# A fused attention and MLP kernel: the first two blocks of v loaded in rows of two tokens and put apart on VectorE, with a new plan of the instruction order

## The chip, the core and the metric

The kernel runs on one core of one Trainium2 chip. The metric is the device time of one execution in microseconds (us). Engines: PE is TensorE, DVE is VectorE, ACT is ScalarE, POOL is GpSimd, SP is SyncE. Loads that change fp32 to fp16 on their way are issued by POOL; SP and ACT issue loads and stores that keep the type.

## The reference, cut to what matters

```
q, k, v: (4 batches, 8 heads, 768 tokens, 64) fp32
scores = q k^T / 8; keep key j for query i if j < 4 (a "sink") or 0 <= i - j < 128
a = softmax over the kept keys;  x = a v, heads side by side: (3072 tokens, 512)
h = x w_in              (512 x 2048)
g = h * sigmoid(1.702 h)
out = g w_out           (2048 x 512), fp32
```

## The kernel before, in words

The 3072 tokens are cut into twelve blocks k of 256 tokens, three to a batch. Of each block the work goes through these stages, four head pairs p at a time where heads matter.

- Loads. q and k of block 0 come by SP and ACT and those of block 1 by SP (`load_cast`, L517), in fp32; copies on DVE, ACT or POOL then cast them to fp16. All later q and k come cast by POOL's loads (`load_rounded`, L434). v is loaded by POOL (L458), the weights w_in and w_out by POOL too (`weights`, L394): w_in in four slices of 512 columns, w_out in four of 512 rows. Slices 0 and 1 of w_in come in two halves of the contracted dimension (`HALVED`).
- `front`: transposes of q and k on PE (L555), a copy of them to `qkT` (DVE or ACT), the few sink rows of k copied into `ks16` (L305 by the helper `copy`), and the scores against the sinks on PE (L585) with their exponentials `ats` on ACT (L593). The sink rows of v go to `vs16`.
- `scores`: products on PE (L695), exponentials `at` on ACT (L724), a mask by DVE (L742, L738), or for four of the first eight pairs a bias added on PE (L678).
- `back`: the products with v, here called av (L770, L775), 1/sum (`rcp`, L790) and scaling (`xn`, L792) on DVE, a transpose (L803) and a copy to `xT`.
- `mm1`: x w_in on PE (L843) into one bank for each slice s of 256 columns of h, tanh on ACT (L857), and on DVE the product `gT` (L859), which frees the bank. At most three such banks are in use. In blocks 0 and 1 and the slices that come in halves, the products with the first half of w_in for both 128 columns come first.
- `mm2`: g w_out, for block 0 plainly (L1021) and from block 1 on by a scheme of seven products (L920), for which `sums` forms sums of w_out on DVE. Results are put together in `osb` (L945, L947) and stored by SP.

The order of the instructions on each engine is not that of the code: `Plan.run` makes it beforehand. Every operation has a duration for each engine that may run it, a due time (`prio`), the operations that it waits for, and sometimes a place in PSUM that it must acquire; the planner then sets one operation after another, on the engine that could end it first. Loads have an order of their own, a list of names:

```python
LOADS = ["a0", "a1", "v0", "b1", "v1", "w0", "w1", "a2", "w2", "w3", "v2", "w4", "w6", "w5", "w7"]
```

Here a and b are q and k (b1 the second half of block 1's), v is v, w0 to w3 w_in and w4 to w7 w_out. Each engine works through its queue in order. A load on POOL also takes one of eight completion counters in turn (`LANES`), so its issue waits until the load eight before it has landed. The second half of block 1's q and k is held back by a small POOL memset (`go`, L495) which stands after v of block 0. Until 12 us PE runs products of zeros where it has nothing else (L1089).

v of a block lies in SBUF as `v16`: 128 partitions, two groups j of 128 tokens, eight heads. Even tokens of a group are in partitions 0 to 63 and odd ones in 64 to 127. Each of the four loads of a block moves one group's even or odd tokens, rows of one token and head: 64 fp32 read, 64 fp16 written.

Of the kernel before, what the change touches and what calls it, by code (L numbers as in the profile page):

```python
# [10 lines left out]
FP16 = mybir.dt.float16  # L11
# [3 lines left out]
P = 128  # L15
D = 64
TB = 256
# [27 lines left out]

BEGIN = 850.0

LATE, LATE_FROM = 500.0, 40000.0
PATIENCE, SLACK = 4000.0, 300.0

SHARED = ("mask", "sum", "wt", "cqk", "ks")
ENGINES = ("PE", "ACT", "DVE", "POOL", "SP")
# [2 lines left out]
class Plan:  # L55
# [4 lines left out]
    def op(self, eng, dur, lat, fn, deps=(), prio=0.0, acq=None, rel=(), kind=""):  # L60
        return self.any({eng: (dur, lat)}, lambda _: fn(), deps, prio, acq, rel, kind)
# [143 lines left out]
def kernel(  # L205
# [11 lines left out]
    nc = tc.nc  # L217
    B, H, S, Dh = q.shape
# [13 lines left out]

    SEVEN_FROM, SEVEN_TO = 1, NK

    EARLY = {1: 4, 2: 5, 3: 0}
    HALVES_FROM, HALVES_X_FROM = 4, 3
    V1_BEHIND = None

    SPLIT_TO = 1

    ROUNDED_FROM = 2, 2
    GO1 = None, 1
    VS_ON, VS_AT = "DVE ACT", 12000.0
    QK_NS, V_NS = 1000, 300
    NH = NF // 2
    HM = d_model // 2

# [3 lines left out]
    def ring(name, n, shape, dt):  # L251
        return [pool.tile(list(shape), dt, name=f"{name}{i}") for i in range(n)]
# [15 lines left out]
    qk32 = ring("qk32", RS, (P, 4 * H * D), FP32)  # L268
    qk16 = ring("qk16", RQ, (P, 4 * H * D), FP16)
    v16 = ring("v16", RV, (P, 2, H, EV), FP16)  # L270
    qkT = ring("qkT", RKT, (P, 2, 2, NP, P), FP16)
    at = ring("at", RA, (P, 2, 512), FP16)
    ats = ring("ats", RA, (P, TB), FP16)
# [4 lines left out]
    gT = ring("gT", RG, (P, NF, TB), FP16)  # L278
    sm = ring("sm", RSM, (P, 4, NH, P), FP16)
    osb = ring("osb", RO, (P, d_model), FP32)  # L280
    bank = [psp.tile([P, 512], FP32, name=f"bank{i}") for i in range(8)]

    plan = Plan(8, {"s": 6, "k": 1, "t": 2, "a": 2, "x": 2, "h": RTH, "o": 3})
    op = plan.op
# [10 lines left out]
    def pick(ns, engs):  # L295
        return {e: ns[e] for e in engs.split()}
# [7 lines left out]
    def copy(e, out, in_):  # L304
        {"POOL": nc.gpsimd.tensor_copy, "DVE": nc.vector.tensor_copy, "ACT": nc.scalar.copy}[e](out=out, in_=in_)  # L305
# [48 lines left out]
    o_ones = op("DVE", 250, 350, ones, prio=NEVER + 1, kind="const")  # L354

    o_ks0, o_vs0 = [], []
    for b in range(B):
# [7 lines left out]
        prio = 24000.0 + 300.0 * b if b else NEVER + 0.5  # L365
# [4 lines left out]

    COPY = ["DVE ACT"] * NK

    KS_ON = "POOL ACT", "POOL"

    ISSUE = 700
    o_win, o_wout, o_w = {}, {}, []

    HALVED = 2
    loads = []

    def weights(j, at):
# [18 lines left out]
            (o_win if j < 4 else o_wout)[2 * (j % 4) + n] = got if j < 4 else o_l  # L400

    L = 16600.0
    LOADS = ["a0", "a1", "v0", "b1", "v1", "w0", "w1", "a2", "w2", "w3", "v2", "w4", "w6", "w5", "w7"]

    SLABS = (0, 1, 4, 5, 2, 3, 6, 7)

    def load_at(x):
        if x in LOADS:
            return NEVER + 10 * LOADS.index(x) + 3
        return 10000.0 + (int(x[1:]) - 3) * L + (0.6 if x[0] == "v" else 0)  # L410

    def nominal(k, slot):
        return 9000.0 + k * L + slot * L / 8

    def attention(k, slot):

        return nominal(k - 1, slot) - EARLY.get(k, 0) * L / 8

    o_cqk, o_cv, o_vs, o_T = {}, {}, {}, {}

    def load_rounded(k, es, war):

# [3 lines left out]
        c16 = qk16[k % RQ].rearrange("p (i e h d) -> p i e h d", i=2, e=2, h=H)  # L426
        n = 2 if k <= SPLIT_TO else 1
        for c in range(n):
# [14 lines left out]
    def load(k):  # L443
        b, r = divmod(k, R)
        t0 = r * TB
        war = reuse("qk16", k % RQ)
        if k < max(ROUNDED_FROM):
            load_cast(k, [e for e in range(2) if k < ROUNDED_FROM[e]], war)
        load_rounded(k, [e for e in range(2) if k >= ROUNDED_FROM[e]], war)
        w16 = v16[k % RV]  # L450

        war = reuse("v16", k % RV) + ([o_ks[0, V1_BEHIND]] if k == 1 and V1_BEHIND is not None else [])

        o_cv[k] = []
        for j in range(2):
            for i in range(2):
                src = v[b, :, t0 + P * j : t0 + P * j + P].rearrange("h (a i) d -> i a h d", i=2)[i]
                o = op("POOL", ISSUE, (430 if k < 2 else V_NS,), lambda i=i, j=j, src=src: nc.gpsimd.dma_start(  # L458
                    w16[64 * i : 64 * i + 64, j, :, 0:D], src), war + [o_ones],
                       prio=load_at(f"v{k}"), kind="load")  # L460
                if not loads:
                    o.behind = o_mask0
                loads.append(o)
                o_cv[k].append(o)
        if r == 0:

            o_vs[b] = []
            for t in range(2):
                for i in range(2):
                    to = vs16[64 * t + 32 * i : 64 * t + 32 * i + 2, b, :, i]  # L470
                    fr = w16[64 * t : 64 * t + 2, 0, i::2, 0:E]
                    deps = [o_cv[k][t], o_vs0[b]]
                    if b:
                        o = op("SP", 450, (20,), lambda to=to, fr=fr: nc.sync.dma_start(to, fr), deps,
                               prio=nominal(k - 1, 0), kind="vs")
                    else:

                        o = plan.any(pick({"POOL": (400, 500), "DVE": (220, 320), "ACT": (420, 540)}, VS_ON),
                                     lambda eng, to=to, fr=fr: copy(eng, to, fr), deps, prio=VS_AT, kind="ks")
                    o_vs[b].append(o)  # L480
                    uses("v16", k % RV, o)

    def load_cast(k, es, war16):
        b, r = divmod(k, R)
        sl = k
        t0 = r * TB
        prio = load_at(f"a{k}")
        war = [], []
        if k:

            for c, g in enumerate(GO1):
                if g is None:
                    continue
                h = c * H // 2 * 2 * D
                go = op("POOL", 80, 180, lambda h=h: nc.gpsimd.memset(qk32[sl][0:1, h : h + 1], 0.0),  # L495
                        prio=load_at("b1" if c else "a1") - 0.2, kind="go")
                go.behind = o_cv[0][g]
                war[c].append(go)
        dst = qk32[sl].rearrange("p (e h i d) -> p e h i d", e=2, h=H, i=2)
        lq = {}  # L500
        if k == 0:
            for p in range(NP):
                for e, (eng, dma, src) in enumerate((("SP", nc.sync, q), ("ACT", nc.scalar, k_ap))):
                    def f(p=p, e=e, dma=dma, src=src):
                        dma.dma_start(  # L505
                            dst[:, e, 2 * p : 2 * p + 2],
                            src[b, 2 * p : 2 * p + 2, t0 : t0 + TB].rearrange("h (p i) d -> p h i d", i=2),
                        )
                    lq[p, e] = op(eng, 500, (560,), f, prio=NEVER + 2.5 + p / 8, kind="load")
        else:  # L510
            n = 2
            for c in range(n):
                hs = slice(c * H // n, (c + 1) * H // n)
                for e in es:
                    src = (q, k_ap)[e]
                    def f(e=e, src=src, hs=hs):
                        nc.sync.dma_start(  # L517
                            dst[:, e, hs], src[b, hs, t0 : t0 + TB].rearrange("h (p i) d -> p h i d", i=2)
                        )
                    o = op("SP", 450, (1800 / n,), f, war[c], prio=load_at("b1" if c else "a1") + 0.1 * e, kind="load")  # L520
                    loads.append(o)
                    for p in range(c * NP // n, (c + 1) * NP // n):
                        lq[p, e] = o
        c16 = qk16[k % RQ].rearrange("p (i e h d) -> p i e h d", i=2, e=2, h=H)
        w = 2 if k == 0 else 4
        for h0 in range(0, H, w):
            for e in es:
                def f(eng, h=slice(h0, h0 + w), e=e):
                    copy(eng, c16[:, :, e, h].rearrange("s i h d -> s h i d"), dst[:, e, h])

                ps = range(h0 // 2, (h0 + w) // 2)
                o = plan.any(cast(P * w, "DVE ACT" if not k else "DVE ACT POOL"), f, [lq[p, e] for p in ps] + war16,
                             prio=nominal(k - 1, -7 + h0) if k else NEVER + h0, kind="cqk")
                for p in ps:
                    o_cqk.setdefault((k, p), []).append(o)
# [214 lines left out]
    def back(k, p):  # L750

        b, r = divmod(k, R)
        u = NP * k + p
        base = attention(k, 2 * p)
        h8 = L / 8
# [22 lines left out]
        dur = 2 * 57 + 8 * 31 if r else 6 * 31  # L778
        deps = [*o_m[k, p], *o_cv[k]] + ([o_se[k, p], *o_cv[k - 1], *o_vs[b]] if r else [])
        rc, X = rcp[u % RR], xn[k % RXN]  # L780
        if p == 0:
            o_xT["war", k] = reuse("xT", k % RX)
            o_xT["warn", k] = reuse("xn", k % RXN)
        o_a = op("PE", dur, dur + 166, av, deps, prio=base - 2 * h8, acq=("a", 1), kind="av")
        uses("at", u % RA, o_a)
        if r:
            uses("ats", u % RA, o_a)
# [12 lines left out]
        def xt():  # L800
            ps = f16(o_x)[:, 0:TB].rearrange("d (j s) -> d j s", j=2)
            for j in range(2):
# [3 lines left out]
                 acq=("x", 1), kind="xt")  # L806
        uses("xn", k % RXN, o_x)

        def cx(e):
            to, fr = xT[k % RX][:, p], f16(o_x)[:, 0:TB]  # L810
            if k == NK - 1:
# [6 lines left out]
                               prio=base - 0.8 * h8, rel=[(o_x, 0)], kind="cx")]  # L818
# [311 lines left out]
```

## Time and profile before

| what | us |
|---|---|
| median of 3 runs | 217.72 (217.53 to 218.18) |
| the profiled execution | 218.23 |
| its span, first to last instruction | 216.2 |
| PE busy in it | 210.8 |
| DVE busy | 185.4 |
| ACT busy | 133.1 |
| POOL busy | 86.0 |

The profile is of one execution. A line of the timeline gives the start, the time until the end, the engine, the source line, the operation, what it writes and reads, and the sizes; in brackets stands how long the engine idled before it and what ended that. A line "xN" merges N instructions. PE's matmuls overlap in their pipelines, so their times add up to more than PE's throughput needs. POOL's time holds its DMA issues (L458, L394, L434), 0.7 to 0.9 us each. In the list of DMA issues the last number is the time from issue to landing.

### The profile page before, as it was taken

How to read it: one execution, taken by the hardware profiler on the slowest of the kernel's cores; microseconds unless marked ns; L12 is line 12 of the kernel's file. 1: busy time of each engine (PE TensorE's matmuls, PEld its weight loads, DVE VectorE, ACT ScalarE, POOL GpSimd, SP SyncE). 2: the span in 40 equal slices, each digit the busy share in tenths (PEclk: the TensorE clock that was granted, in tenths of full speed). 3: DMA queues.
4: the chain of work that ended last, by engine and by line, in shares of the span. 5: the costliest groups of instructions: out<-in, count | busy, mean ns of one | idle time of the engine just before them, and what ended most of it. 6: DMA issues, size and time to landing. Idle time of an engine off the chain costs nothing.

```text
span 216.2 us, 6592 instructions
## 1 busy us (share of the span) xinstructions
PE 210.8 (97%) x2680; PEld 181.0 (84%) x2680; DVE 185.4 (86%) x429; ACT 133.1 (62%) x277; POOL 86.0 (40%) x136
## 2 busy tenths in 40 slices
PE   7899999999999999999999999999999999999994
PEld 7568887678888988988888988888889889888883
DVE  5698899998988988988988979889979879878674
ACT  3867695366686775765675775864675865744330
POOL 7979564499996260699300080540000000000000
PEclk9999999999999999999999999999999999999999
DMA  6999999999999498099970099091040031022042
GB/s 179 215 196 179 200 192 205 168 163 166 108 167 165 30 144 77 5 133 170 89 124 3 0 96 125 5 114 36 3 97 3 0 76 28 0 52 49 2 100 97
DMA packets 79734, 21.41 MB, mean 99 GB/s; under 512 B 68184, under 2 KB 76888, under 8 KB 79704
## 3 DMA queue, kind: packets, MB, share of 16 engines
q0 software_dynamic: 71200, 12.59, 73.2%
q1 hardware_dynamic: 7416, 7.88, 13.5%
q10 hardware_dynamic: 1088, 0.52, 0.8%
q8 instruction: 21, 0.34, 0.7%
q14 instruction: 9, 0.07, 0.1%
HBM read 27.26 MB, written 6.29 MB: 155 GB/s over the span
## 4 chain that ended last, share of the span: by engine, by line
PE 92%; DVE 3%; DMA 2%; ACTq 1%; issue 0%
PE bank L843 39%; PE bank L920 31%; PE bank L695 5%; PE bank L775 5%; PE bank L1021 3%; DMA qk<-in_k_dram 2%; PE bank L618 2%; PE bank L770 2%; PE bank L585 2%; PE bank L555 1%; DVE osb L947 1%; PE bank L642 1%; PE bank L803 1%; ACTq L505 1%; PE bank L678 1%; DVE xn L792 1%
## 5 line engine op out<-in xcount | busy, mean ns | idle before, releaser
L843 PE MATMUL bank<-xT,w_in 128*128 128x256 f16 x768 | 103.7, 273 | 0.0
L857 ACT ACTIVATE th<-bank 128x512 f16<-128x512 f32 x96 | 57.6, 604 | 57.9 <-PE bank L843 51.6
L843 PEld LDWEIGHTS <-w_in 128*128 128x128 f16 x768 | 71.9, 98 | 8.9
L859 DVE SCALAR_TENSOR_TENSOR gT<-th,bank 128x512 f16<-128x512 f16 x96 | 64.9, 678 | 10.1 <-ACT th L857 9.8
L724 ACT ACTIVATE at<-bank 128x512 f16<-128x512 f32 (+1 forms) x96 | 49.1, 584 | 1.5 <-PE bank L695 1.1
L458 POOL DMA_DIRECT2D v<-in_v_dram x48 | 33.2, 719 | 30.4 <-PE bank L775 24.8
L920 PEld LDWEIGHTS <-sm 128*128 128x128 f16 x352 | 33.3, 98 | 4.2 <-issue 0.2
L920 PE MATMUL bank<-wt,sm 128*128 128x256 f16 x264 | 36.1, 273 | 0.0
L947 DVE SCALAR_TENSOR_TENSOR osb<-bank,osb 128x256 f32<-128x256 f32 x58 | 23.9, 417 | 11.8 <-PE bank L920 11.8
L920 PEld LDWEIGHTS <-gT 128*128 128x128 f16 x264 | 25.5, 98 | 3.4
L920 PE MATMUL bank<-w_out,gT 128*128 128x256 f16 x176 | 26.1, 273 | 0.0
L738 DVE TENSOR_TENSOR at<-at,mask 128x1024 f16<-128x1024 f16 x30 | 20.5, 683 | 0.2 <-ACT at L724 0.2
L792 DVE TENSOR_TENSOR xn<-bank,rcp 128x256 f16<-128x256 f32 x48 | 20.0, 417 | 0.6
L775 PE MATMUL bank<-v,at 128*128 128x65 f16 x352 | 20.0, 193 | 0.0
L434 POOL DMA_DIRECT2D qk<-in_q_dram x20 | 18.0, 925 | 0.6 <-DMA qk<-in_q_dram 0.5
L434 POOL DMA_DIRECT2D qk<-in_k_dram x20 | 18.0, 923 | 0.7 <-PE bank L843 0.5
L775 PEld LDWEIGHTS <-at 128*128 128x128 f16 x352 | 17.4, 97 | 0.9
L305 POOL COPY ks<-qkT 64x4 f16<-64x4 f16 x26 | 8.1, 313 | 18.6 <-DVE qkT L305 17.6
L890 DVE TENSOR_TENSOR sm<-gT 128x1024 f16<-128x1024 f16 x22 | 15.0, 680 | 0.1
L593 ACT ACTIVATE ats<-bank 128x256 f16<-128x256 f32 x32 | 13.0, 405 | 1.7 <-PE bank L585 1.6
L945 ACT ACTIVATE osb<-bank 128x256 f32<-128x256 f32 x22 | 8.4, 382 | 9.1 <-PE bank L920 9.1
L695 PE MATMUL bank<-qkT 64*128 64x256 f16 x192 | 13.3, 244 | 0.0
(58 smaller groups left out, 224.0 us busy)
## 6 DMA issues: line engine op xcount, KB each, us to landing
out_dram<-osb SPq DMA_DIRECT2D x48, 128.0 KB
v<-in_v_dram POOLq DMA_DIRECT2D x48, 64.0 KB, 5.1
qk<-in_q_dram POOLq DMA_DIRECT2D x20, 128.0 KB, 5.4
qk<-in_k_dram POOLq DMA_DIRECT2D x20, 128.0 KB, 5.6
w_out<-in_moe_w_out_dram POOLq DMA_DIRECT2D x4, 512.0 KB, 11.3
w_in<-in_moe_w_in_dram POOLq DMA_DIRECT2D x4, 256.0 KB, 6.6
w_in<-in_moe_w_in_dram POOLq DMA_DIRECT2D x2, 512.0 KB, 8.9
qk<-in_k_dram ACTq DMA_DIRECT2D x4, 128.0 KB
```

The costliest lines, as they stand in the source:

```text
L434: nc.gpsimd.dma_start(c16[:, i, e, hs], src[b, hs, t0 : t0 + TB].rearrange("h (p i) d -> i p h d", i=2)[i])
L458: o = op("POOL", ISSUE, (430 if k < 2 else V_NS,), lambda i=i, j=j, src=src: nc.gpsimd.dma_start(w16[64 * i : 64 * i + 64, j, :, 0:D], src ...
L695: nc.tensor.matmul(f32(o_b or o_s, 2 * n + i)[:, c : c + w].rearrange("s (j t) -> s j t", t=P), src[d, j, 1, p], T[d, j0:j1, 0, p], start= ...
L724: nc.scalar.activation(out=A[:, i, 0:W], in_=f32(o_b or o_s, 2 * n + i)[:, 0:W], func=AF.Exp, scale=scale)
L738: nc.vector.tensor_tensor(out=a_, in0=a_, in1=m_[:, 2 * P :].unsqueeze(1).to_broadcast((P, 4, 2 * P)), op=ALU.mult,)
L775: nc.tensor.matmul(avp()[:, j, i], A[:, i, c : c + P], src[:, jj, 2 * p + i, 0:E], start=not r and n == 0, stop=n == len(blocks) - 1, skip ...
L792: o_nn = op("DVE", 333, 425, lambda: nc.vector.tensor_tensor(out=X[:, p].rearrange("s j (h d) -> s j h d", h=2), in0=avp()[:, :, :, 0:D], ...
L843: nc.tensor.matmul(f32(holder[0])[:, bass.ts(e, TB)], w_in16[:, c, bass.ts(Fi, P)], X[:, c], start=(c == 0 and not (halved and e)), stop=( ...
L857: o_t = op("ACT", 477, 600, lambda first=first: nc.scalar.activation(out=th[first.places[0]], in_=f32(first), func=AF.Tanh, scale=0.851), ...
L859: o_g[k, s] = op("DVE", 595, 690, lambda first=first, s=s: nc.vector.scalar_tensor_tensor(out=g[:, 2 * s : 2 * s + 2].rearrange("p a t -> ...
L920: nc.tensor.matmul(f32(holder[bank_of])[:, 0:HM], x[:, Fi], w[:, Fi], start=first and Fi == 0, stop=Fi == NH - 1, skip_group_check=True)
L947: f, ns = (lambda: nc.vector.scalar_tensor_tensor(out=out, in0=src(), scalar=0.5, in1=add, op0=ALU.mult, op1=ALU.add)), (333, 425)
```

## The change

- v of blocks 0 and 1 (`V2_TO = 2`) is loaded into a tile `v2`, two loads a block, each of four heads and all 256 tokens: partition p takes tokens 2p and 2p+1, a row of 128 fp32 read and 128 fp16 written. Four copies a block, planned on DVE (`CV_ON`), then put the rows of v2 into v16 as it was.
- The `go` memset stands behind the second load of v of block 0, which is now the last.
- Slices 0, 1 and 2 of w_in come in halves, not 0 and 1 alone; slice 2 is loaded ahead of q and k of block 2.
- The sink rows of k of batch 0 may be copied by DVE or ACT (were POOL or ACT), those of v by POOL, DVE or ACT (were DVE or ACT).
- Some of the planner's numbers are others: `LATE`, `PATIENCE`, `SLACK`, `EARLY`, `VS_AT`, the due time of av. `SPLIT_TO` has no effect, since blocks 0 and 1 do not pass through its loop.

```diff
-LATE, LATE_FROM = 500.0, 40000.0
-PATIENCE, SLACK = 4000.0, 300.0
+LATE, LATE_FROM = 1000.0, 40000.0
+PATIENCE, SLACK = 2000.0, 100.0
...
-    EARLY = {1: 4, 2: 5, 3: 0}
+    EARLY = {1: 4, 2: 5, 3: 2}
...
-    SPLIT_TO = 1
+    V2_TO = 2
+    CV_ON, CV_AT = "DVE", -9000.0
+
+    SPLIT_TO = 0
...
-    VS_ON, VS_AT = "DVE ACT", 12000.0
+    VS_ON, VS_AT = "POOL DVE ACT", 9000.0
+    V2_NS = 650, 750
+    v2 = ring("v2", V2_TO, (P, H, 2 * D), FP16)
...
-    KS_ON = "POOL ACT", "POOL"
+    KS_ON = "DVE ACT", "POOL"
...
-    HALVED = 2
+    HALVED = 3
...
-    LOADS = ["a0", "a1", "v0", "b1", "v1", "w0", "w1", "a2", "w2", "w3", "v2", "w4", "w6", "w5", "w7"]
+    LOADS = ["a0", "a1", "v0", "b1", "v1", "w0", "w1", "w2", "a2", "w3", "v2", "w4", "w6", "w5", "w7"]
...
+        o_cv[k], o_lv[k] = [], []
+        if k < V2_TO:
+            for c in range(2):
+                hs = slice(c * H // 2, (c + 1) * H // 2)
+                src = v[b, hs, t0 : t0 + TB].rearrange("h (p i) d -> p h (i d)", i=2)
+                o = op("POOL", ISSUE, (V2_NS[k],), lambda hs=hs, src=src: nc.gpsimd.dma_start(v2[k][:, hs], src),
                        prio=load_at(f"v{k}"), kind="load")
...
+                o_lv[k].append(o)
+        for j in range(2):
+            for i in range(2):
+                if k < V2_TO:
+                    to = w16[64 * i : 64 * i + 64, j, :, 0:D]
+                    fr = v2[k][64 * j : 64 * j + 64].rearrange("p h (i d) -> p h i d", i=2)[:, :, i]
+                    o = plan.any(pick({"POOL": (570, 670), "DVE": (340, 440), "ACT": (490, 600)}, CV_ON),
+                                 lambda eng, to=to, fr=fr: copy(eng, to, fr), war + [o_ones, *o_lv[k]],
+                                 prio=CV_AT if k == 0 else nominal(0, 0) + CV_AT - 9000.0 + 1000.0, kind="cqk")
+                    o_cv[k].append(o)
+                    continue
...
-                go.behind = o_cv[0][g]
+                go.behind = o_lv[0][g]
...
-        o_a = op("PE", dur, dur + 166, av, deps, prio=base - 2 * h8, acq=("a", 1), kind="av")
+        o_a = op("PE", dur, dur + 166, av, deps, prio=base - 1 * h8, acq=("a", 1), kind="av")
```

The order of the instructions that the planner makes of it differs at the start on every engine. Of block 0 and 1's work: all four ks pairs are on DVE (three were on ACT, one on POOL); one vs copy is on DVE, one on ACT and two on POOL (four on DVE); two of block 1's four qkT copies are on ACT (all on DVE); and the last cast of block 1's k is on DVE (POOL). On PE the first halves of the products L843 for s = 0 and 1 of block 0 stand ahead of the last two of block 0's transposes to `xT`, and twelve more L843 products stand ahead of block 2's transposes. From about 50 us on, the two orders differ in the place of av among the other products; the last groups are the same.

More of the change, by code (lines that the diff above doesn't have):

```diff
@@ L417, in attention @@
         return nominal(k - 1, slot) - EARLY.get(k, 0) * L / 8
-    o_cqk, o_cv, o_vs, o_T = {}, {}, {}, {}
+    o_cqk, o_cv, o_lv, o_vs, o_T = {}, {}, {}, {}, {}
     def load_rounded(k, es, war):
@@ L452, in load @@
         war = reuse("v16", k % RV) + ([o_ks[0, V1_BEHIND]] if k == 1 and V1_BEHIND is not None else [])
[L454 to L459, printed above, removed]
+        o_cv[k], o_lv[k] = [], []
[4 more added lines that the diff above has]
+                o = op("POOL", ISSUE, (V2_NS[k],), lambda hs=hs, src=src: nc.gpsimd.dma_start(v2[k][:, hs], src),
                        prio=load_at(f"v{k}"), kind="load")
@@ L463, in load @@
                 loads.append(o)
+                o_lv[k].append(o)
[9 more added lines that the diff above has]
+                    continue
+                src = v[b, :, t0 + P * j : t0 + P * j + P].rearrange("h (a i) d -> i a h d", i=2)[i]
+                o = op("POOL", ISSUE, (V_NS,), lambda i=i, j=j, src=src: nc.gpsimd.dma_start(
+                    w16[64 * i : 64 * i + 64, j, :, 0:D], src), war + [o_ones],
+                       prio=load_at(f"v{k}"), kind="load")
+                loads.append(o)
                 o_cv[k].append(o)
+                o_lv[k].append(o)
         if r == 0:
```

## The prediction

> **What bounds it now.** I read the busy table first, then the stages, then the start.
>
> ```profile
> PE 210.8 (97%) x2680; PEld 181.0 (84%) x2680; DVE 185.4 (86%) x429; ACT 133.1 (62%) x277; POOL 86.0 (40%) x136
> PEclk9999999999999999999999999999999999999999
> ```
>
> The busy time by stage (us in the stretch, busy and count per engine, granted clock, DMA share, GB/s written):
>
> ```profile
> 12.00:18.00 6.00, 5.60 (x95) 3.76 (x93) 5.13 (x20) 4.62 (x13) 4.80 (x7) 1.00 1.49 191
> 18.00:22.00 4.00, 4.00 (x55) 3.59 (x53) 3.96 (x12) 2.73 (x6) 4.00 (x6) 1.00 2.18 166
> 22.00:28.00 6.00, 6.00 (x70) 5.16 (x69) 4.75 (x11) 4.32 (x10) 2.95 (x5) 1.00 1.44 197
> 28.00:50.00 22.00, 22.00 (x222) 16.47 (x221) 21.76 (x55) 14.11 (x31) 14.42 (x19) 1.00 1.74 181
> 50.00:200.00 150.00, 150.00 (x2013) 132.65 (x2012) 131.68 (x290) 95.89 (x195) 49.72 (x79) 1.00 0.72 73
> ```
>
> From 18 us on PE never rests and the clock is full: that work is the same before and after, so the end moves only if PE's dense part starts earlier or later, or gets holes. "Busy" flatters PE before 18 us, since it counts pipeline time. Counting columns (256 in 0.109 us, four matmuls in 0.44 by the chain), real work up to 18.07 us is 8.3 us, and holes from 12 to 18 us are about 1.9 us. That is the room. DVE is near full from 9 to 22 us: whatever is added there counts.
>
> The chain of waits through the start shows who sets it:
>
> ```profile
> 2.39 5.13 DMA qk<-in_k_dram
> ...
> 13.97 0.33 DVE xn L792
> 14.30 0.20 DVE xT L305
> ...
> 15.59 0.34 DVE qkT L305
> 15.94 0.05 issue
> ...
> 18.07 0.44 PE bank L843 x4
> ```
>
> DMA until 7.5 us, then DVE and PE in turn, until the first product with w_in (L843). The timeline of ACT (start, us, engine, line):
>
> ```profile
> 13.38 0.38 ACT L593 ACTIVATE ats<-bank 128x256 f16<-128x256 f32 x1 [1.63 <-PE bank L585]
> 13.70 1.08 ACT L724 ACTIVATE at<-bank 128x512 f16<-128x512 f32 x2
> 19.10 0.60 ACT L857 ACTIVATE th<-bank 128x512 f16<-128x512 f32 x1
> ```
>
> and POOL's:
>
> ```profile
> 14.40 0.60 POOL L305 CAST qk<-qk 128x512 f16<-128x512 f32 x1 [1.20 <-DMA qk<-in_k_dram]
> ```
>
> ACT idles 1.63 us before 13.38 and then runs almost without a gap to 19.1. POOL, not DVE, waits for the last half of block 1's k.
>
> **Loads.** Eight v issues become four: 4 x 0.71 us (L458) less on POOL. The pair of ks copies there (0.67) leaves too, so the first w_in issue moves from 10.38 to about 6.8. That hardly matters by itself: w_in's first half was issued at 10.38 and took 5.7 us to land (16.1), queued behind v and qk. The DMA engines are the limit. From 20 to 22 us, when rows of 128 B (written) flow alone, the DMA view shows 163 GB/s; from 30 to 38 us, with 1024-B rows, 207. A v block writes 256 KB, 1.61 us at the first rate and 1.27 at the second; rows of 256 B lie between, nearer the first (estimate 1.5). Two blocks: 0 to 0.7 us, I take 0.2. The Trainium skill (DMA: Bandwidth & Descriptors, Specifications) puts the line rate at rows of at least 512 B; the write side here stays at 256 B, so by it v lands as late as now and the sum below would not change. No run yet shows 256-B rows.
>
> The "go" memset follows two v issues instead of four (6.59 to about 5.2), so SP asks for block 1's second half at 5.5 instead of 6.85. Its k, issued at 7.27, lands about 7.0 us later now (14.3, just before POOL's cast at 14.40). Issued at about 5.9, that would be 12.9; but v and w_in, now ahead on POOL's queue, take more of the engines meanwhile, so anything up to 15 is possible, and I take 13.8. v0 landed at 11.5 (last issue 5.85 plus 5.6); now about 10.5. w_in halves follow every 1.27 us from about 14.5 to 20.8 for all six, then block 2's qk by 24.3 (3.4 us for four, as now). None is the last to come: first use of w_in is at 16.1 below, slice 2 at 22.9, block 2's transposes at 26.9. So the load gains are hidden. Two more half issues on POOL (0.7 each) are hidden by the eight loads in flight; w_in's slice ahead of block 2's qk costs its consumers nothing while those 2.6 us stand.
>
> **Copies.** Added on DVE: eight v copies of 512 f16 per lane. Rows: the bias TENSOR_SCALAR 128x512 f16 takes 0.29 and the next starts 0.21 later; the fp32 CAST 128x512 is 0.40, next 0.31 to 0.38 later. They are like the first in type, so 0.21 each and 0.84 a block. The dear end is 0.40, the step of the three vs copies that ran beside POOL's w_in issues (10.65 to 11.88; a fourth, at 12.34, took a step of 0.25). At 0.40, block 0's copies end 0.75 later, of which 0.5 hides behind the k cast below, block 1's another 0.75, and 0.3 of slack on DVE remains: 0.25 + 0.75 - 0.3 = 0.7 more. The Trainium skill (SBUF — State Buffer, SBUF: two separate sides) says that a DVE copy in a two-port mode and a GpSimd operation exclude each other for a whole instruction, which speaks against copies on DVE: block 1's four meet POOL's issues of block 2's qk (0.91 each), and one full wait of 0.9 there would be 0.6 past the slack. The 0.40 rows bear out some wait, not a full one.
>
> Also added: four ks pairs (0.2 each by the 0.07 MEMSET 128x16 rows and a wait; 0.15 to 0.4), and one 512 cast (0.38). Removed: three of four vs copies (1.20 for three) and two qkT copies (0.34 each). DVE net: 1.7 + 0.8 + 0.4 - 1.2 - 0.7 = +1.0, up to +2.5. ACT loses three ks pairs (1.2 us) but in time where it later idles 1.63; it gains two qkT copies (0.58 each) and one vs (0.45), and the second qkT falls inside its gapless run.
>
> **The new chain.** From the instruction orders, with start-to-start times of the rows (exp pair 0.97, ats 0.31, xT 0.27 on ACT; mask 0.7, xn 0.35, xT 0.2, rcp 0.1, gT 0.66 on DVE; av of a pair 0.36, L843 0.44 a half on PE):
> ACT: qkT of block 1's pair 1 at 12.25 (its transposes follow the k cast at 11.0), vs to 13.2, then ats, at, ats, at to 15.8, xT 16.0, qkT of pair 3 to 16.6, ats, at to 17.9, ats, half at, xT 18.9, half at 19.4. The old run ended at 19.1.
> DVE: v0 copies 11.95 to 12.8, cast, vs, then the k cast, which now waits in DVE's own queue, with all of block 0's normalizing behind it: 13.8 to 14.2; rcp and xn of pairs 0, 1 to 15.3, qkT, xT 15.8, v1 copies to 16.7, xn of pairs 2, 3 to 17.6. The mask needs ACT's 17.9; then mask, rcp, xn, rcp, xT, xn, xT, mask, rcp, xT, xn to 21.3, and the first gT (L859 now) ends at 21.95.
> PE: L843's first halves need only xT of pairs 0, 1: 16.1 and 17.0 (after ACT's qkT), then xt and two av to 18.3. By then it has done 0.87 us of L843 more and 0.22 of transposes less than now at 18.07: 0.65 - 0.26 = **0.39 us gained**. Then holes: 0.27 for block 1's first xn (19.1), 0.1 for the second mask (20.65), 0.4 for the first gT, because L843 may hold three banks and all three slices begun early hold one until gT frees it (21.95): **0.77 us lost**. From 22 us PE is dense again (each further gT comes 0.1 to 0.9 us ahead of need). Block 2's transposes would start at 26.9 with twelve more L843 (1.31 us) ahead of them, against 25.24: +0.35 to +0.38.
>
> The rest of the replan (LATE, PATIENCE, SLACK, EARLY, av's priority) shifts av by one group in each block of the steady part and leaves the last 3 us in the same order. PE waits for nothing there, so 0, at most 0.3 either way; if av came too late, xn and then L843 would be next.
>
> **Sum.** The profiled execution is 218.23 us (span 216.2), 0.51 above the median 217.72. 218.23 - 0.39 + 0.77 = 218.6; from the median, 218.1. Its bounds: dear copies, 0.7 more (218.8); the steady part, 0.3 less, and cheaper copies nothing, as ACT's 17.9 then holds the mask; a gT that comes a third earlier gives back 0.3 (217.5).
>
> **Rivals.** *Faster:* DVE is no longer slowed by POOL. Single steps vary beside POOL's issues: a CAST 128x256 took 0.29 at 3.66 and 0.57 at 7.54, a CAST 128x512 0.40 to 0.45. In the new order POOL issues nothing from about 11 to 13 us. If the twenty DVE steps from 10 to 18 us each lose 0.04, DVE and, behind its copies, ACT come 0.8 earlier, the 0.77 goes, and more of the 1.9 us of holes fills: against the sum 0.8 to 1.5 gained, 216.6 to 217.3, likeliest 216.9. Against: ACT's gapless run starts only 0.2 earlier than the old one.
> *Slower:* the k cast in DVE's queue. Slack from 17.6 to 17.9 covers a landing up to 14.1; beyond, each us counts. w_in's large rows now compete with that half, so 14.6 to 15 is possible: 0.5 to 0.9 more, 218.6 to 219.0. For it: from 10 to 14 us the DMA engines are full in the page's slices (9 in all of them). The same sign: POOL's second vs copy stands behind block 2's k issue, which waits for w_in's first landing; decisive only past 16.0.
> *The change does not do what it says:* v lands no sooner. Then 218.1 all the same, since no load is last.
>
> **Numbers.** A measurement here tells about 0.3% (0.65 us) from no change. The forecast 218.1 with its bounds (217.5 to 218.8) has 0.45, of which 0.10 is past 218.4; the faster rival has 0.29, of which 0.02 falls short of 0.3%; the slower one 0.26. So faster by over 0.3% 0.27, within it 0.35 + 0.02 = 0.37, slower 0.36. Range 216.9 to 219.0: it cuts half of the faster rival (0.13) and the worst of the slower (0.05).
>
> **What would show it.** Right: DVE's copies near 0.29 each; first L843 near 16.1; PE waiting near 19 and 22 us for xn and gT; first gT about 22; steady part with no new waits. Wrong: POOL's or DVE's cast of block 1's k after 14.5 us (slower), the first gT before 21 (faster), or any new PE wait after 30 us.

## The result, and the profile after

Six runs of the changed kernel gave a median of 219.63 us (218.83 to 220.47), six of the kernel before 217.91 (217.53 to 218.37). The ratio is 1.0075 (95% interval 1.0052 to 1.0098): slower by 1.7 us, where 218.1 was forecast and the range ended at 219.0. The profiled execution took 220.47 us (span 218.7), the slowest of the six, so its rows overstate the difference a little. The page:

```profile
PE 211.8 (97%) x2679; PEld 181.5 (83%) x2679; DVE 189.9 (87%) x441; ACT 133.2 (61%) x274; POOL 82.7 (38%) x132
PEclk9999999999999999999999999999999999999999
```

The stages of the changed kernel, with the columns as in the view of before:

```profile
12.00:18.00 6.00, 4.73 (x71) 3.01 (x70) 5.82 (x16) 4.44 (x12) 4.22 (x6) 1.00 1.27 205
18.00:22.00 4.00, 3.29 (x54) 2.42 (x54) 3.88 (x14) 2.66 (x7) 2.21 (x4) 1.00 1.75 183
22.00:28.00 6.00, 6.00 (x67) 5.44 (x65) 5.81 (x15) 3.99 (x7) 3.60 (x5) 1.00 1.85 180
28.00:50.00 22.00, 22.00 (x230) 16.12 (x228) 21.45 (x54) 14.10 (x31) 14.22 (x20) 1.00 1.72 177
50.00:200.00 150.00, 150.00 (x2016) 132.66 (x2017) 132.21 (x290) 96.70 (x198) 48.67 (x78) 1.00 0.72 73
```

From 22 us on nothing has changed: PE is busy throughout, and in this execution most of DVE's `gT`, to the last one, end some 2.4 us later than before. From 12 to 22 us PE is busy 8.02 us, where before it was 9.60. Most of the loss is there. The chain of waits through that stretch (start, us, what):

```profile
12.24 0.27 DVE v L311
...
13.17 0.40 DVE v L311
...
13.61 0.89 DVE qk L311
14.51 0.67 DVE vs L311
15.21 0.44 DVE qk L311
...
15.69 0.57 PE bank L578 x7
...
17.42 0.75 DVE v L311
18.19 0.29 DVE v L311
18.49 0.61 DVE v L311
...
19.89 0.29 PE bank L826 x2
```

The v copies are now links of the chain, in both blocks; in the chain of before PE and DVE took turns there. Between the two groups stand a cast of 0.89 us and a vs copy of 0.67. DVE's and POOL's timelines (start, us, engine, line; xN merges N) show what they met:

```profile
12.24 1.33 DVE L311 COPY v<-v 64x512 f16<-64x512 f16 x4
13.61 0.87 DVE L311 CAST qk<-qk 128x512 f16<-128x512 f32 x1
14.51 0.67 DVE L311 COPY vs<-v 2x260 f16<-2x260 f16 x1
15.21 0.43 DVE L311 CAST qk<-qk 128x512 f16<-128x512 f32 x1
16.96 2.14 DVE L311 COPY v<-v 64x512 f16<-64x512 f16 x4
```

```profile
13.37 1.76 POOL L440 DMA_DIRECT2D qk<-in_q_dram  x2
15.95 0.87 POOL L440 DMA_DIRECT2D qk<-in_k_dram  x1 [0.82 <-DMA w_in<-in_moe_w_in_dram]
16.87 0.40 POOL L311 COPY vs<-v 2x260 f16<-2x260 f16 x1
17.21 0.87 POOL L440 DMA_DIRECT2D qk<-in_k_dram  x1
18.25 0.75 POOL L400 DMA_DIRECT2D w_in<-in_moe_w_in_dram  x1 [0.17 <-issue]
```

The cast at 15.21 met no issue and took 0.43; an equal cast at 13.61, beside POOL's issues of block 2's q, took 0.87. Block 0's four copies took 1.33 together: three stood alone, the last beside POOL's vs copy at 12.91 (0.40 for 0.29). Block 1's took 2.14, one by one 0.45, 0.75, 0.29 and 0.61: the first began beside POOL's vs copy of 16.87, the second beside the k issue of 17.21, the fourth beside the w_in issue of 18.25; the third was not held. ACT, which ran almost without a gap to 19.1 before, now waits for PE:

```profile
16.89 0.37 ACT L311 COPY xT<-bank 128x256 f16<-128x256 f16 x1 [1.00 <-PE bank L826]
```

### The profile page after: what moved, and what is told of

It reads as the page before. It is cut to its first block, busy times and chain, and to the rows that moved or that the text cites. A ratio compares the mean times of both kernels' runs of the same rounds, so it can differ in the third digit from the quotient of the medians.

```text
span 218.7 us, 6608 instructions
## 1 busy us (share of the span) xinstructions
PE 211.8 (97%) x2679; PEld 181.5 (83%) x2679; DVE 189.9 (87%) x441; ACT 133.2 (61%) x274; POOL 82.7 (38%) x132
## 4 chain that ended last, share of the span: by engine, by line
PE 91%; DVE 5%; ACT 1%; ACTq 1%; issue 1%; DVEq 0%
PE bank L866 38%; PE bank L943 30%; PE bank L718 5%; PE bank L798 5%; PE bank L1044 3%; PE bank L578 2%; PE bank L641 2%; PE bank L793 2%; PE bank L608 1%; DVE v L311 1%; PE bank L826 1%; DVE qk L311 1%; DVE osb L970 1%; ACTq L528 1%; PE bank L665 1%
## 5 line engine op out<-in xcount | busy, mean ns | idle before, releaser
L866 PE MATMUL bank<-xT,w_in 128*128 128x256 f16 x768 | 102.1, 273 | 0.0
L482 POOL DMA_DIRECT2D v<-in_v_dram x40 | 27.8, 722 | 37.1 <-PE bank L798 29.0
L943 PEld LDWEIGHTS <-gT 128*128 128x128 f16 x264 | 24.9, 98 | 3.2
L440 POOL DMA_DIRECT2D qk<-in_k_dram x20 | 17.9, 920 | 1.8 <-DMA w_in<-in_moe_w_in_dram 0.8
L311 POOL COPY ks<-qkT 64x4 f16<-64x4 f16 x24 | 6.2, 259 | 18.4 <-DVE qkT L311 16.7
L943 PE MATMUL bank<-wt,gT 128*128 128x256 f16 x88 | 13.0, 272 | 0.0
## 6 DMA issues: line engine op xcount, KB each, us to landing
w_out<-in_moe_w_out_dram POOLq DMA_DIRECT2D x4, 512.0 KB, 10.5
```

Of the source, the lines that this page charges most:

```text
L440: nc.gpsimd.dma_start(c16[:, i, e, hs], src[b, hs, t0 : t0 + TB].rearrange("h (p i) d -> i p h d", i=2)[i])
L482: o = op("POOL", ISSUE, (V_NS,), lambda i=i, j=j, src=src: nc.gpsimd.dma_start(w16[64 * i : 64 * i + 64, j, :, 0:D], src), war + [o_ones], ...
L866: nc.tensor.matmul(f32(holder[0])[:, bass.ts(e, TB)], w_in16[:, c, bass.ts(Fi, P)], X[:, c], start=(c == 0 and not (halved and e)), stop=( ...
L943: nc.tensor.matmul(f32(holder[bank_of])[:, 0:HM], x[:, Fi], w[:, Fi], start=first and Fi == 0, stop=Fi == NH - 1, skip_group_check=True)
```

## The experiments

Each ratio is to the kernel before, run beside it on the same chip; 0.001 is 0.22 us. An issue is POOL's instruction that starts a transfer; a VectorE instruction that runs while POOL issues is said to meet it.

**What single instructions cost.** A kernel of nothing but runs of equal instructions, first alone, then beside four transfers issued by POOL.

> A measurement of single instructions; it leaves out everything that the reference computes and its time means nothing. Runs of equal instructions, each first alone and then beside four transfers issued by GpSimd: v copies (64x512 f16, SBUF to SBUF) on VectorE, casts of 128x512 from fp32, copies of 128x512 f16 from PSUM, products 128x1024 f16, and the v copies on ScalarE. Shared port: the v copies take 0.2 to 0.3 us alone and 0.4 to 0.6 or single ones up to 0.9 beside the issues, the casts 0.3 to 0.4 alone and 0.6 to 0.9 beside; copies from PSUM, products and ScalarE's copies do not change. Added work: each kind takes the same alone and beside, the v copies 0.3 or more already alone. A stretch of all kinds alike would speak for traffic of the landing data rather than for the issues.

The groups by line (shortest, median, longest ns). v copies, casts and copies from PSUM come first alone and then beside the issues; products and the v copies on ACT are shown beside the issues only (alone their medians were 692 and 614):

```profile
L61 DVE COPY dst<-src x8: 272/288/292, 4.9 to 7.1; 64x512 f16<-64x512 f16 x8
L61 DVE COPY dst<-src x10: 277/290/614, 8.0 to 12.0; 64x512 f16<-64x512 f16 x10
L72 DVE CAST cst<-fsrc x6: 419/426/428, 13.5 to 15.8; 128x512 f16<-128x512 f32 x6
L72 DVE CAST cst<-fsrc x5: 419/841/866, 16.6 to 19.5; 128x512 f16<-128x512 f32 x5
L76 DVE COPY pcp<-bank x6: 417/424/424, 22.2 to 24.5; 128x512 f16<-128x512 f16 x6
L76 DVE COPY pcp<-bank x8: 419/424/425, 25.4 to 28.6; 128x512 f16<-128x512 f16 x8
L80 DVE TENSOR_TENSOR bigo<-big,msk x5: 683/691/693, 32.7 to 35.6; 128x1024 f16<-128x1024 f16 x5
L67 ACT COPY dst<-src x6: 612/616/617, 39.6 to 42.8; 64x512 f16<-64x512 f16 x6
```

Alone, eight copies follow each other every 0.32 us (4.91 to 7.46), not every 0.21. Beside issues, four of the twelve (ten are in the row) took 0.54 to 0.61, one for each issue, so an issue costs a copy some 0.27; casts went from 0.43 to as much as 0.87. What reads PSUM, the product of two operands and ACT's copies take the same beside issues as alone, and the copies were back at 0.29 from 11.64 us on, right after the last issue, though its data landed until 18.8: so this is no slowing by landing data. Both halves of the expectation hold: the copy is dearer alone than the forecast had it, and dearer again in company.

**Which issues, which instructions.**

> A second measurement of single instructions; it leaves out everything that the reference computes and its time means nothing. V copies of 64x512 on VectorE beside GpSimd's issues of w_in (0.71 us each, large rows) and beside six small copies of GpSimd's own (2x260); f16 arithmetic on one operand (128x512) and small copies (2x260) on VectorE, alone and beside issues of q. If GpSimd's writing of descriptors holds VectorE's SBUF path: each issue costs a copy 0.15 to 0.3, the shorter w_in issue no more than q's; one-operand arithmetic is held as well (0.29 alone, 0.57 beside), small copies too (0.22 alone, 0.47 beside). If it is the landing data instead: w_in's large rows cost nothing, and the stretch goes on after the last issue.

One-operand arithmetic alone and beside q issues, then small copies likewise:

```profile
L79 DVE TENSOR_SCALAR cst<-pcp x4: 286/294/295, 15.8 to 16.8; 128x512 f16<-128x512 f16 x4
L79 DVE TENSOR_SCALAR cst<-pcp x6: 285/414/540, 17.5 to 19.7; 128x512 f16<-128x512 f16 x6
L83 DVE COPY vsm<-vsr x4: 209/218/218, 21.6 to 22.4; 2x260 f16<-2x260 f16 x4
L83 DVE COPY vsm<-vsr x6: 208/348/615, 23.0 to 24.9; 2x260 f16<-2x260 f16 x6
```

As expected, both are held by q issues: by 0.25 the arithmetic, by 0.26 to 0.39 the small copies, which gain nothing from being short. An issue of w_in of 128x2x512 (0.72 us) held a v copy by 0.07 to 0.13 here, and each of POOL's own small copies held one by 0.09 to 0.13. The stretch ended with the last issue. In the kernels w_in's issues held more: in the changed kernel two ks copies took 0.47 and 0.50 for some 0.16 beside them, and the last v copy 0.61 for 0.29, there beside the issue of a whole slice.

**The old loads of v in the new plan.** `-    V2_TO = 2` `+    V2_TO = 0`

> The changed kernel with blocks 0 and 1's v loaded as before (four transfers a block, no copies); everything else of the replan kept. The changed kernel is 1.7 us over the kernel before (219.63 against 217.91). Three theories share that out. Shared port (VectorE's SBUF-to-SBUF copies and casts are stretched while GpSimd issues transfers; eight more such copies stand in VectorE's queue in the first 20 us): without the copies nearly all of it comes back, 217.5 to 218.4. Added work (the eight copies cost what they cost wherever they stand): the same, 217.5 to 218.4; this run does not tell these two apart. Replan (the new order, the ks copies on VectorE, the early slices): nearly nothing comes back, 219.2 to 219.8. In between, 218.5 to 219.1, both have a part.

218.35 us, 1.0021 (1.0005 to 1.0038). Rows and copies are most of the loss. What is left, 0.2%, the new plan has without them.

**The new rows in the old plan.** Every setting of the planner, the order of loads and of halves as before; only the v loads and copies are new.

> The kernel before with the new v loads and the eight copies alone; the planner's settings, the ks copies on GpSimd and ScalarE, the vs copies and w_in's order are those of before. Shared port, and added work: slower than before by most of the 1.7 us, 218.7 to 219.6. Replan: about as before, 217.6 to 218.2. By the shared port alone, the copies of block 1 show a mean near 0.5 us, those of block 0 near 0.3.

220.24 us, 1.0107 (1.0088 to 1.0127), beyond the expected range: by the medians the new plan is worth 0.3% to a kernel that has the copies, though the two intervals overlap. Block 1's copies did not show 0.5 each but 1.42 for four: there one of them (0.53) met an issue of w_in and the others none; the long waits of PE for the casts of k (2.3 us) stand here too.

**The same transfers and order, no copies.** The products read v of blocks 0 and 1 from v2, which makes part of the result another:

```diff
-                                 lambda eng, to=to, fr=fr: copy(eng, to, fr), war + [o_ones, *o_lv[k]],
+                                 lambda eng: None, war + [o_ones, *o_lv[k]],
...
-        vt, vp = v16[k % RV], v16[(k - 1) % RV]
+        vt, vp = [v16[x % RV] if x >= V2_TO else v2[x] for x in (k, max(k - 1, 0))]
```

> The changed kernel with the same transfers and every engine's other instructions in the same order, but the eight v copies are left out: the products read v of blocks 0 and 1 where the transfers put it, with tokens in another order than the reference has (every lane reads its second token in both halves), so that part of the result is another. Two memsets of about 0.1 us are added before 3.9 us. Copies as the cause (their own length of 0.32 each and their meeting with GpSimd's issues): the whole difference to the version with old v loads comes back, 217.6 to 218.4. Late start as the cause (the version with short copies began 1.36 us later on VectorE and took 0.9 more than the changed kernel, so it said nothing of the copies): not in question here. Loads or the new order as the cause: 219.2 to 219.8.

218.58 us, 1.0021 (1.0001 to 1.0041): what the copies cost is the whole difference to the version with the old loads, so the new transfers themselves cost and gain nothing that these runs can tell (0.2%). Its stages:

```profile
12.00:18.00 6.00, 5.82 (x85) 3.82 (x84) 3.82 (x15) 5.55 (x15) 3.83 (x6) 1.00 1.28 205
18.00:22.00 4.00, 4.00 (x70) 3.59 (x68) 3.89 (x13) 2.74 (x7) 2.25 (x5) 1.00 1.70 183
```

PE is busy 9.82 us of these ten, DVE from 12 to 18 us 3.82 instead of 5.82. DVE's timeline:

```profile
13.50 0.47 DVE L311 CAST qk<-qk 128x512 f16<-128x512 f32 x1 [0.69 <-DMA qk<-in_k_dram]
...
17.78 0.69 DVE L763 TENSOR_TENSOR at<-at,mask 128x1024 f16<-128x1024 f16 x1 [1.40 <-ACT at L749]
```

The last cast of k now waits for its landing and the mask for ACT; with the copies both stood behind DVE's own queue, at 15.21 and 20.08.

**A wait that was none.** Block 2's q and k were made to depend on block 1's copies, in the plan: `load_rounded(k, ..., war + (o_cv[1] if k == 2 else []))`.

> The changed kernel with one more dependence: GpSimd issues block 2's q and k only after block 1's four v copies on VectorE are done. The same instructions, nearly the same order; only the meeting of these copies with GpSimd's issues is gone. Shared port: block 1's copies at about 0.3 us each instead of 0.54, the wait of TensorE near 20 us shorter by 0.7 to 1.1, time 218.4 to 219.0. Added work: copies as long as before, time 219.4 to 219.9. Replan: 219.4 to 219.9 too. If block 2's q and k, now about 1 us later, are late for their transposes near 27 us, a new wait of TensorE stands there and the time is 219.6 or more under all three.

219.66 us, 1.0080 (1.0057 to 1.0102). The waits on the chip come from what instructions read and write, not from the plan's list, and POOL issued block 2's q at 13.30 as ever; the edit only put one vs copy ahead of an issue. So it is no test of the meeting, but stands nearly as a repeat of the changed kernel. Its profiled execution, the fastest of its six (218.97), tells something else: block 1's copies met one issue in it and took 1.46 instead of 2.14, since POOL issued at other moments. How many meetings there are differs from execution to execution.

**A true wait.** POOL copies one element of v16 of block 1 into block 2's q tile, which the load then overwrites:

```diff
+            hold = op("POOL", 120, 220, lambda: nc.gpsimd.tensor_copy(
+                out=qk16[k % RQ][64:65, 0:1], in_=v16[1][64:65, 1, 0, 0:1]), war + o_cv[1], prio=load_at("a2") - 0.2, kind="go")
```

> The changed kernel with a true wait this time: GpSimd copies one element of v of block 1 into block 2's q tile (overwritten by the load) before it issues block 2's q and k, so that these issues come after block 1's v copies. DVE's order up to the first mask is that of the changed kernel. Meeting (VectorE's SBUF copies and casts are held up by GpSimd's issues, in the measurement of single instructions by 0.27 us each for a v copy and 0.43 for a cast of 512): block 1's copies 0.32 each instead of 0.54, the casts of k 0.43 instead of 0.87, 1.3 us less on VectorE; of that 0.7 to 1.2 reach the end, time 218.4 to 218.9. Length alone (the copies' 0.32 each cost the time wherever issues stand): 219.4 to 219.9. If block 2's q and k come too late, a wait of TensorE for their transposes after 26 us shows, and the time is 219.6 or more.

218.94 us, 1.0052 (1.0033 to 1.0070). DVE's timeline:

```profile
13.60 0.56 DVE L311 CAST qk<-qk 128x512 f16<-128x512 f32 x1
14.19 0.22 DVE L311 COPY vs<-v 2x260 f16<-2x260 f16 x1
14.44 0.43 DVE L311 CAST qk<-qk 128x512 f16<-128x512 f32 x1
...
16.20 1.19 DVE L311 COPY v<-v 64x512 f16<-64x512 f16 x4
```

The same instructions in the same order, without the issues: 0.56 for 0.87, 0.22 for 0.67, 1.19 for 2.14. The wait moved more than block 2's issues: POOL's second vs copy now stands at 13.48, where the cast of 0.56 meets it, and the issue of w_in that follows at 21.4. So what is gone is block 1's meeting with all of POOL's work. PE still waits 0.8 us for casts of k, 0.6 of it for the last, which stands behind copies of plain length. No late wait for block 2 appears.

**The share of each.** The wait and the changed kernel side by side, and the wait without copies.

> The changed kernel itself, beside the version with the wait. It was 1.0075 of the kernel before (1.0052 to 1.0098), and a version that differed from it only in the place of one small copy 1.0080. Both theories: 1.006 to 1.009.

> The version with the wait and the copies, beside the changed kernel. Meeting as the larger share of the 1.2 us: 1.003 to 1.004, nearer to the version without copies. Own length as the larger share: 1.006 to 1.007, nearer to the changed kernel. About half each: 1.0045 to 1.0055, as in its first measurement.

> The version without the eight copies (1.0021 of the kernel before), with a true wait: GpSimd issues block 2's q and k only after VectorE's last cast of block 1's k. Of the computation it leaves out what that version leaves out. Without copies the casts of that stretch took 0.42 to 0.47, so hardly any instruction is left that such issues could hold: if only the meeting matters, as without the wait, 1.001 to 1.003. If later issues of block 2's q and k are a gain in themselves (less traffic in the way of w_in and of block 1): 0.998 to 1.000. If they are a loss: 1.004 or more, and the meeting's share is then larger than the version with wait and copies shows.

The changed kernel 1.0089 (1.0055 to 1.0123), with the wait 1.0036 (1.0009 to 1.0063), with the wait and no copies 1.0008 (0.9989 to 1.0027). Over both measurements the changed kernel has 1.0082, the wait 1.0044: 0.0038, or 0.8 us, for the meeting. From 1.0044 to 1.0008 lie another 0.8 us for the copies' own length, or 0.5 if the version without a wait (1.0021) is the foot. So about half each; with intervals of 0.2 to 0.3% the runs do not divide it finer. Of the 0.2% left without copies they do not show whether it is real in each version. The wait gains nothing that can be told where there are no copies (1.0008 against 1.0021), so later issues are no gain in themselves that these runs can tell.

The repeat of the changed kernel shows a third thing. In its profiled execution, the slowest of its six (221.61), block 1's last k landed only at 16.18, not at 13.25 as in the first profile. DVE idled 1.54 us before its cast at 16.21, PE stood 2.0 us for it, and the granted clock was then 0.50 from 17.4 to 20.9 us. In the other profiles of both kernels and their versions that k landed between 13.08 and 14.31. How often it comes late is not shown.

**Block 0 alone.** `-    V2_TO = 2` `+    V2_TO = 1`

> The changed kernel with the new v rows and copies for block 0 alone; block 1's v loaded as before by four transfers. Between the version without new v rows (218.35) and the changed kernel (219.63) lie 1.3 us. Meeting: block 0's copies stand in a stretch in which GpSimd issues nothing, block 1's beside issues; block 0 has the smaller share, 218.5 to 218.9. Length alone: half each, 218.9 to 219.2. Loads and waits: block 0's share is the larger, 219.2 to 219.6.

218.92 us, 1.0053 (1.0031 to 1.0074), at the edge between two of the expectations and about half of the whole. Block 0's copies took 1.39 us with only issues of w_in beside them. How they cost it is open: PE waits 1.1 us for the last cast of k, but in this execution that cast waited for its landing at 14.25, after DVE had idled 0.48 us, and not for the copies.

**The copies on ACT.** `-    CV_ON, CV_AT = "DVE", -9000.0` `+    CV_ON, CV_AT = "ACT", -9000.0`

> The changed kernel with the eight v copies on ScalarE, where in the measurement of single instructions a copy takes 0.62 us, the same alone and beside GpSimd's issues. VectorE is relieved of 2.6 to 3.5 us, ScalarE gets 5 us in a stretch in which it runs with few gaps. Meeting or length on VectorE as the cause: VectorE's waits go, but ScalarE's exp come later by up to 2.5 us a block; 218.8 to 220.0, with TensorE's waits now for ScalarE. Loads and waits as the cause: 219.5 to 221. If it comes below 218.5, ScalarE had room that the prediction did not see.

220.40 us, 1.0131 (1.0095 to 1.0167): a little beyond the range for copies as the cause, and inside the range for loads and waits, so the time alone does not speak for the copies. ACT's timeline:

```profile
11.67 2.54 ACT L311 COPY v<-v 64x512 f16<-64x512 f16 x4
...
16.38 2.51 ACT L311 COPY v<-v 64x512 f16<-64x512 f16 x4
```

They are not held there, but twice as long, and each group stops the exponentials for 2.5 us. PE waited for ACT, as foretold (0.4 us twice), and 1.2 us in all for `xn`.

**The cast of k on POOL, with the true wait.** `"POOL" if h0 and e else "DVE ACT POOL"` as the engines of a cast of block 1.

> The version with the true wait (block 2's q and k issued after block 1's v copies, 218.94) with one more edit: the cast of the second half of block 1's k stands on GpSimd, as in the kernel before, and no longer in VectorE's queue behind block 0's copies and a vs copy. TensorE's waits for that cast near 14.5 and 15.2 us were 0.21 and 0.66. VectorE's queue as the cause of that rest: those waits shrink by 0.4 to 0.6, 218.3 to 218.7. If the cast is held by the landing of k or by GpSimd's own speed (0.60 for it in the kernel before): 218.8 to 219.2.

219.57 us, 1.0057 (1.0038 to 1.0076), above both expected ranges: no gain over the wait alone. The waits from 12 to 22 us (us in total, times, longest):

```profile
PEld L830 <- DVE xn L819: 2.2, 4, 1.3
```

PE no longer waits for the cast but for `xn`, which stands behind the same copies in DVE's queue. That reads as the length of that queue and not the cast's place in it, though PE's order is another here too.

**Short copies, an experiment that failed.** Each copy moves one head instead of eight, and two memsets fill the rest.

> The changed kernel, every engine's instructions in the same order, but each of the eight v copies moves one head of eight (64x64 instead of 64x512); seven heads of v of blocks 0 and 1 are left out of the result, and their place is filled with ones by two longer memsets on VectorE in its idle time before 3.9 us. Same loads, same waits, same number of instructions: only the copies' length is gone, about 0.25 us of each. Copies' length on VectorE (alone or beside GpSimd): 217.7 to 218.4, nearly all of the difference to the kernel without the new v loads (218.35) or more. Loads and waits (copies as one more stop between landing and use, new transfers): 219.3 to 219.8 as the changed kernel. Replan: 219.3 to 219.8.

220.55 us, 1.0126 (1.0102 to 1.0150). The memsets of ones took 1.34 us each, and DVE's first cast began at 5.27 instead of 3.91:

```profile
2.36 1.34 DVE L358 MEMSET v<- 128x1536 f16 x1 [0.27 <-issue]
...
13.73 0.88 DVE L311 COPY v<-v 64x64 f16<-64x64 f16 x4
```

So it says nothing of the copies' share: the late start and the shorter copies together came to 0.4 to 0.5% over the changed kernel, and what each did is not shown. One thing can be read from it: a copy of an eighth of the length still takes 0.16 to 0.18 where nothing meets it, and 0.29 to 0.44 beside POOL's work.

**An attempt at something faster.** The kernel before with `VS_ON = "ACT"`.

> The kernel before, with the four small vs copies on ScalarE (about 0.4 each, in its idle 1.6 us before 13.4) and none on VectorE, where three of them stood beside GpSimd's w_in issues and took 0.47 instead of 0.22. An attempt at a version that beats both. If VectorE's queue from 10.6 to 12.5 us sets the start: 0.3 to 0.8 gained, 217.1 to 217.6. If ScalarE's products behind the copies set it: 217.8 to 218.4. If neither: as before, 217.9.

218.03 us, 0.9993 (0.9977 to 1.0008): no difference, though the order changed in more than these copies (the last cast of k came to DVE). So there is no sign that DVE's queue from 10.6 to 12.5 us sets the start of the kernel before. No version here beats it.

## Why the prediction was wrong

The step that failed is a term of the sum: "so 0.21 each and 0.84 a block", and with it the dear end of 0.40. Four copies took a step of 1.36 us in block 0 and 2.17 in block 1 (to the next instruction's start), so 0.34 and 0.54 each, where 0.40 was to be the worst.

- *The cheap end misread a row.* 0.21 was the time from one instruction to a different one that started over it. A run of equal copies goes at 0.32, which is the 0.29 of the row and a little more.
- *The dear end mixed two prices.* The step of 0.40 was a mean over vs copies of before of which two took 0.47, beside issues, and one 0.22. So a meeting costs 0.25 on top of whatever the copy costs. Added to 0.32 that is 0.57; in the measurement of single instructions a copy beside a q issue took 0.54 to 0.61. Block 1's mean of 0.54 is no such price but made of 0.45, 0.75, 0.29 and 0.61. The surcharge was in the rows behind the prediction (its cast of 0.57 for 0.29 at 7.54 shows it too), and was taken for a step.
- *The meeting was charged to the v copies alone.* A cast (0.87 for 0.43) and a vs copy (0.67 for 0.22) in the same queue were left at their old prices, though POOL's issues of q had moved onto them. By steps: 1.36 for 0.84, 0.90 for 0.38, 0.70 for 0.25 and 2.17 for 0.84, together 2.8 us more on DVE. Taken through the prediction's own sum (0.5 hidden, 0.3 of slack) that is an estimate of 2.0 us, in an execution 0.8 us slower than the median; the median came 1.5 over the forecast. The copies were to meet block 2's q and k; of block 1's four one met such an issue, one POOL's vs copy and one w_in's issue. The kernel before has only PSUM readers on DVE while block 2's q and k are issued.

**The weighed rule.** The Trainium skill (SBUF — State Buffer, SBUF: two separate sides) spoke against the copies, and rightly; the prediction gave it a part of the range and no case of its own. The trace agrees on who is held (0.43 to 0.87 for the cast, 0.424 both times from PSUM, 0.69 for the product beside issues). It does not agree that it is for the whole instruction of POOL: an issue of 0.88 held one copy by 0.27 and let another run beside it in 0.29.

**What was right, and what was luck.** Without the copies the chain's moments came out as worked out: first L843 product 15.89 (forecast 16.1), mask 17.78 and held by ACT (17.9), first gT begun at 21.15 and done about 21.8 (21.95). With the copies the same points came at 17.44, 20.08 and about 23.9. That the version without copies is 0.46 us slower than before (interval 0.0 to 0.9), where the sum had 0.38 lost, is luck as far as its trace goes. Counted by columns as in the prediction, PE had done 8.8 us of work by 18 us in it and 12.7 by 22 us, and before 8.7 and 12.7: neither the 0.39 gained nor the 0.77 lost is there, and PE is busy from 18 to 22 us throughout, without a hole of 0.4 for the first gT. In the first profile the loads came near the forecast and were hidden: v0 landed at 10.77 (10.5), block 1's k at 13.25 (13.8); w_in's first half was later than thought (15.66 for 14.5), block 2's q and k came at 26.3 instead of 24.3, and neither PE, DVE nor ACT waited for them. In the repeat's profile v0 landed at 12.14 and that k at 16.18, and it was not hidden. The steady part moved nothing.

**The rivals.** The slower rival had the right place, the cast of k in DVE's queue, and its sign, a cast after 14.5, showed at 15.21 and, in the repeat, at 16.21. Its reason, a late landing, was wrong in the first profile, where DVE's own copies held the cast and k had landed at 13.25, and right in the repeat's. Which of the two holds in the median execution is open. What the medians show is that all of the loss but 0.2% goes when the copies go. The faster rival assumed that DVE is freer because POOL issues nothing from 11 to 13 us. It issues from 13.4 on instead, where the casts and copies now stand. Of PE's waits that were foretold near 19 and 22 us, the first showed, with 0.7 us at 19.89 for 0.27; near 22 us PE was busy throughout. The largest one, 0.9 at 15.69 before block 1's last transposes, was not in the prediction.

## What to carry to other kernels

Price an instruction by a run of its own kind, start to start, and not by the distance to an unlike neighbour. Where copies within SBUF stand on VectorE, lay GpSimd's issues beside them on one timeline and charge each meeting as a surcharge on whichever instruction is there, old ones included: a reordering moves the meetings as well. So does the next execution, so read more than one profile before a wait is called past. A transfer that arrives earlier than anyone needs it pays for nothing that is done to it afterwards.

## What the runs showed of the hardware

In the measurements of single instructions an issue of q by POOL (0.88 us) held a VectorE instruction with one SBUF source by 0.24 to 0.44 us, a copy of 2x260 no less than one of 64x512. An issue of w_in (128x2x512, 0.72 us) held a v copy by 0.07 to 0.13 there, but in the kernels such issues held small copies by 0.25 (before, 0.47 for 0.22) to 0.33 (after, 0.50 for 0.17). The issues of q themselves hardly grew: 0.88 to 0.92, and up to 1.07 for the first of a row. VectorE copies from PSUM (0.424), products of two SBUF operands (0.69) and ACT's copies (0.62) took the same beside issues as alone.
